# Last layer pair in 2x2 blocks with seven block products in place of eight, its weights kept in DRAM

## Chip, core and metric

The kernel runs on one core of a Trainium2 chip. The metric is the device time of one execution in microseconds. The core's engines work side by side and meet by semaphores: TensorE (PE, with its weight load PEld) does the matmuls, VectorE (DVE) and ScalarE (ACT) do elementwise work and empty PSUM, where matmuls leave their sums, GpSimd (POOL) gathers and scatters rows, SyncE (SP) issues most of the DMAs. Each engine takes its instructions in a fixed order.

## What is computed

Attention over 8 batches and 8 heads gives x of 4608 rows (tokens) and 512 columns. A router gives each of 8 experts 576 tokens, and each expert computes `relu(x @ w1[e]) @ w2[e]`. The change concerns the last pair of layers:

```python
def _moe2_ref(x, w1, w2, w3, w_out) -> np.ndarray:
    h = np.maximum(np.maximum(x @ w1, x @ w2), x @ w3)
    return (h @ w_out).astype(np.float32)
```

with w1, w2, w3 of 512 x 768 and w_out of 768 x 512. These four matrices come as 64-bit floats.

## The kernel before

**Split products.** Each fp32 operand is split into a high part of type fp32r and a low part, the rest. A product is three matmuls on TensorE, high·high, low·high and high·low, for each 128 rows of the contraction.

**Stages.** Attention and the first part of the routing take the time to about 210 us. Then the 8 experts run one after another (r = 0 to 7), each with a first matrix (line L891: 8 tiles f of 128 features, in two halves of 288 tokens and 12 matmuls each) and a second (L921: 4 tiles d, 24 matmuls in each half). A tile of the first matrix is emptied by ACT (L900, relu and high part, `hhi`) and DVE (L908, low part, `hlo`). A tile of the second is emptied by ACT into `ys` (L928) and sent to `yd` in DRAM by a DMA that ACT issues (L929). `acc` has two buffers in PSUM, so that tile d+2 can't start before tile d has been emptied. The stage starts for expert 7 at 621.55 us, its second matrix at 646.99 us, and the last layer pair at 672.43 us.

**Last pair.** `yd` is read back in 9 blocks b of 512 tokens (`yload`, L846) and split (`ysplit`, L857). `layer1(b, f)` does the three products of one tile f of 128 features (m = 0, 1, 2 for w1, w2, w3; L974, 12 matmuls of 512 columns each): 9 x 6 x 3 x 12 = 1944 matmuls. Their maximum is taken by ACT (L980) and DVE (L982, L983), and split (L985, L986). `layer2(b, t)` multiplies 128 tokens by w_out (L996, 18 matmuls of 512 columns), 36 x 18 = 648 matmuls, and is followed by a copy (L1000) and a scatter by GpSimd (L1002). The split weights of this stage stay in SBUF, 12 chunks of 1 MB.

**Weights and conversion.** Chunks of weights come from DRAM into `raw` (L657), are split by ACT (L672) and DVE (L679), and lie in a ring of 11. The 64-bit weights are converted on the chip by `convert()`: 24 jobs of 128 x 512 numbers, each an ACT operation (L785), six DVE operations (L788 to L803) and a store to DRAM (L806: `m0` to `m2`, `mo`), from which they come back as ordinary chunks.

**What sets the order.** The order on each engine is written by the program. `pump()`, called after each 6 matmuls of the experts, asks a planner which pending piece of splitting, routing or conversion may come next: a `Clock` counts what is booked on DVE against the time of TensorE, and a conversion step is placed where it fits within a limit. `have(n)` forces chunk n where it is needed.

Of the kernel before, what the change touches and what calls it, by code (L numbers as in the profile page):

```python
# [20 lines left out]
G = NT // 128  # L21
NU = G // 4
# [586 lines left out]
def kernel(ctx, tc, q, k, v, w_gate, w1, w2, m1, m2, m3, m_out, out, mark=lambda n: None):  # L609
# [6 lines left out]
    ms = [dram.tile([DM, F2], F32, name="m%d" % i) for i in range(3)] + [dram.tile([F2, DM], F32, name="mo")]  # L616
# [6 lines left out]
    ring = ctx.enter_context(tc.tile_pool(name="ring", bufs=11))  # L623
    P = rt.W = ctx.enter_context(tc.tile_pool(name="mw", bufs=1))
    PS = ctx.enter_context(tc.tile_pool(name="mps", bufs=2, space=PSUM))
    chunks = []
    todo, inflight, stage = [], [], ["raw%d" % i for i in range(4)]

    for n in stage:
        P.tile([128, 1024], F32, name=n)  # L630
    for n, w in (("xhi", 4), ("xlo", 4), ("hhi", 8), ("hlo", 8)):
        P.tile([128, w, CAP], F32R, name=n)
    NC = 8 * E + 12
# [16 lines left out]
    def issue():  # L650

        n = state["issued"]
        if todo and len(inflight) + len(half) < len(stage) and n - state["used"] < 11 + (n == NC - 1) and state["conv"] >= todo[0][2]:
            ap, a, _ = todo.pop(0)
            raw = P.tile([128, 1024], F32, name=stage[0])
            stage.append(stage.pop(0))
            nc.sync.dma_start(raw.rearrange("p (a f) -> p a f", a=a), ap)  # L657

            inflight.append([raw, clock.pe + (16 if state["issued"] % 8 == 0 else 10) * clock.PLACE])
            state["issued"] += 1  # L660

    def split_hi():
        mark("wsplit")
        raw, _ = inflight.pop(0)
        if state["split"] < NC - 1:
            t = ring.tile([128, 2, 1024], F32R, name="chunk")
            hi, lo = t[:, 0], t[:, 1]
        else:
            while half:
                split_lo()  # L670
            hi, lo = (P.tile([128, 1024], F32R, name="last%d" % i, tag=stage.pop(0)) for i in range(2))
# [32 lines left out]
    def gather(r):  # L704
        mark("gather")
        xg = []
        for t in range(5):
            g = P.tile([128, DM], F32, name="xg", bufs=5)
# [51 lines left out]
    def convert():  # L760


        jobs = [(src[a:a + 128, o:o + 256], dst[a:a + 128, o:o + 256]) for o in range(0, F2, 256)
                for src, dst in zip((m1, m2, m3), ms) for a in range(0, DM, 128)]
        jobs = [jobs[i:i + 2] for i in range(0, len(jobs), 2)]
        jobs += [[(m_out[a:a + 128, :], ms[3][a:a + 128, :])] for a in range(0, F2, 128)]
        raw, there = [], []

        def load(job):
            raw.append(P.tile([128, 512, 2], I32, name="c64", bufs=2))  # L770
            there.append(clock.pe + 10 * clock.PLACE)
            n = 512 // len(job)
            for i, (ap, _) in enumerate(job):
                nc.sync.dma_start(raw[-1][:, i * n:i * n + n].rearrange("p f w -> p (f w)"), ap.bitcast(I32))

        load(jobs[0])
        for i, job in enumerate(jobs):
            yield 270, there[i]
            mark("conv")
            if i + 1 < len(jobs):  # L780
                load(jobs[i + 1])
            hw, lw = raw[i][:, :, 1], raw[i][:, :, 0]
            t = P.tile([128, 512], I32, name="ct", bufs=2)
# [7 lines left out]
            nc.vector.tensor_scalar(t, t, 3, 0x3FFFFFF8, op0=OP.logical_shift_left, op1=OP.bitwise_and)  # L791
            yield 540, 0
# [4 lines left out]
            nc.vector.tensor_scalar(hw, t, -0x800000, None, op0=OP.bitwise_and)  # L797
            yield 540, 0
# [4 lines left out]
            nc.vector.tensor_tensor(tf, ex, tf, op=OP.add)  # L803
            n = 512 // len(job)
            for k, (_, dst) in enumerate(job):
                nc.sync.dma_start(dst, tf[:, k * n:k * n + n])  # L806
            state["conv"] += 2
# [33 lines left out]
    NB = NT // 512  # L841
    YS = {}

    def yload(b):
        t = P.tile([128, 4, 512], F32, name="yraw", tag="aoh")
        nc.sync.dma_start(t, yd[:, b * 512:(b + 1) * 512].rearrange("(a p) t -> p a t", p=128))  # L846
        return t

    def ysplit(b, raw):
        mark("ysplit")  # L850
        if b % 2:
            t = P.tile([128, 2, 4, 512], F32R, name="yodd", tag="hhi")
            YS[b] = t[:, 0], t[:, 1]
        else:
            YS[b] = [P.tile([128, 4, 512], F32R, name="y" + n, tag=n) for n in ("xhi", "xlo")]
        for a in range(4):
            nc.scalar.copy(YS[b][0][:, a], raw[:, a])  # L857
            nc.vector.tensor_tensor(YS[b][1][:, a], raw[:, a], YS[b][0][:, a].bitcast(F32), op=OP.subtract)

# [8 lines left out]
    for r in range(E):  # L868
        if r + 1 == E:
            for i in range(3):  # L870
                for n, m in enumerate(ms[:3]):
                    want(m.rearrange("(a p) f -> p a f", p=128)[:, :, 256 * i:256 * i + 256], 4, 12 * i + 4 * n + 4)
            for i in range(3):
                want(ms[3].rearrange("(a p) f -> p a f", p=128)[:, 2 * i:2 * i + 2, :], 2, 36 + 4 * i + 4)
# [4 lines left out]
        for f in range(8):  # L879
# [4 lines left out]
            for hf in range(2):  # L884
# [21 lines left out]
                if hf == 1:  # L906
# [3 lines left out]
                    clock.book(1, 600)  # L910
        for d in range(4):
# [136 lines left out]
```

## Time and profile before

| | |
|---|---|
| median of 3 runs | 1273.55 us (1272.87 to 1275.11) |
| the profiled execution: its own time | 1270.92 us |
| its span in the trace | 1269.1 us |
| TensorE busy | 1230.4 us, 97% of the span |
| VectorE, ScalarE, GpSimd busy | 51%, 31%, 11% |
| experts, from about 210 us | to 672.43 us |
| last layer pair | 672.43 to about 1260.9 us |

The span is 1.8 us shorter than the profiled execution's own time, and that execution is 2.6 us below the median. The chain of waits shows what ended last at each moment; a timeline shows one engine's instructions by start and length; windows show the busy time of each engine in a stretch. In a timeline a row's length counts the pipeline of the last matmul in it, so the rate of matmuls is read from one row's start to the next.

### The profile page before, as it was taken

The numbers are of one execution on the slowest core, as the hardware profiler recorded it, in microseconds if no ns is written. First come the engines' busy times: TensorE is split into PE (matmuls) and PEld (weight loads), VectorE is DVE, ScalarE is ACT, GpSimd is POOL, SyncE is SP. The second block draws the span as 40 slices with busy tenths as digits, with TensorE's granted clock in tenths as the row PEclk, the third lists the DMA queues.
The fourth block names the chain that finished last, engine by engine and source line by source line (L and its number), as shares of the span: only waits on it lengthen the run. The fifth ranks groups of instructions, "written<-read, shape, count | busy, mean of one in ns | idle before, by whom it ended". The sixth has DMA issues, their size and how long they took to land.

```text
span 1269.1 us, 20900 instructions
## 1 busy us (share of the span) xinstructions
PE 1230.4 (97%) x8585; PEld 1075.4 (85%) x8585; DVE 649.5 (51%) x1359; ACT 398.3 (31%) x622; POOL 143.2 (11%) x239
## 2 busy tenths in 40 slices
PE   5999978999999999999999999999999999999997
PEld 4888855999999999999998888888888888888886
DVE  6888876777778687777664313131313131313121
ACT  4888832233333323354243212021211121212110
POOL 7222211012010010210000010101010101010101
PEclk9999987999999999999999999999999999999999
DMA  9999715364435353585652101010101010100000
GB/s 210 247 252 250 193 51 159 99 188 126 146 124 172 125 172 111 187 277 183 221 177 102 34 34 34 34 34 34 34 34 34 34 34 34 34 34 1 25 9 34
DMA packets 138017, 136.78 MB, mean 108 GB/s; under 512 B 37570, under 2 KB 114626, under 8 KB 137922
## 3 DMA queue, kind: packets, MB, share of 16 engines
q1 hardware_dynamic: 122514, 94.39, 27.2%
q0 software_dynamic: 9984, 31.47, 7.4%
q10 hardware_dynamic: 5424, 9.59, 2.0%
q8 instruction: 68, 1.11, 0.4%
q14 instruction: 27, 0.22, 0.1%
HBM read 100.75 MB, written 34.67 MB: 107 GB/s over the span
## 4 chain that ended last, share of the span: by engine, by line
PE 55%; issue 34%; DVE 6%; POOL 2%; DMA 1%; ACT 1%; POOLq 0%; SPq 0%; DVEq 0%; ACTq 0%
PE acc L921 15%; PE acc L891 14%; PE acc L974 6%; PE pX L166 3%; PE pT L95 3%; PE pc L974 3%; PE pS L116 3%; PE po L996 2%; POOL out_dram L1002 2%; PE pA L153 1%; PE pxt L732 1%; PE pY L184 1%; PE rp L487 1%; PE pL L196 1%; DVE hlo L908 1%
## 5 line engine op out<-in xcount | busy, mean ns | idle before, releaser
L921 PE MATMUL acc<-hhi,chunk 128*128 128x288 f32 x1024 | 212.8, 301 | 0.0
L891 PE MATMUL acc<-xhi,chunk 128*128 128x288 f32 x1024 | 204.9, 300 | 2.2 <-DVE hlo L908 1.3
L891 PEld LDWEIGHTS acc<-xhi,chunk 128*128 128x128 f32 x1024 | 160.3, 188 | 3.8 <-DVE hlo L908 2.3
L921 PEld LDWEIGHTS acc<-hhi,chunk 128*128 128x128 f32 x1024 | 162.6, 188 | 0.1
L982 DVE TENSOR_TENSOR tb<-ta,acc 128x512 f32<-128x512 f32 x54 | 37.1, 687 | 234.0 <-ACT ta L980 233.9
L921 PE MATMUL acc<-hlo,chunk 128*128 128x288 f32 x512 | 150.9, 295 | 0.1
L974 PE MATMUL acc<-yxhi,chunk 128*128 128x512 f32 x480 | 147.8, 389 | 0.0
L891 PE MATMUL acc<-xlo,chunk 128*128 128x288 f32 x512 | 143.1, 295 | 0.0
L974 PE MATMUL acc<-yodd,chunk 128*128 128x512 f32 x576 | 134.4, 389 | 0.0
L974 PEld LDWEIGHTS acc<-yodd,chunk 128*128 128x128 f32 x576 | 108.1, 188 | 22.5
L1002 POOL DMA_INDIRECT out_dram<-ot,ia x36 | 34.6, 962 | 673.9 <-DVE ot L1000 621.0
L974 PEld LDWEIGHTS acc<-yxhi,chunk 128*128 128x128 f32 x480 | 90.1, 188 | 18.8
L679 DVE TENSOR_TENSOR chunk<-raw,chunk 128x1024 fp32r<-128x1024 f32 x75 | 91.0, 1218 | 23.8 <-ACT chunk L672 23.4
L921 PEld LDWEIGHTS acc<-hlo,chunk 128*128 128x128 f32 x512 | 96.0, 188 | 0.3 <-DVE hlo L908 0.3
L980 ACT COPY ta<-acc 128x512 f32<-128x512 f32 x54 | 31.7, 586 | 204.6 <-PE acc L974 202.5
L891 PEld LDWEIGHTS acc<-xlo,chunk 128*128 128x128 f32 x512 | 93.4, 188 | 0.0
L974 PE MATMUL acc<-yxlo,chunk 128*128 128x512 f32 x240 | 93.4, 389 | 0.0
L900 ACT ACTIVATE hhi<-acc 128x576 fp32r<-128x576 f32 x64 | 41.8, 653 | 140.4 <-PE acc L891 125.5
L672 ACT CAST chunk<-raw 128x1024 fp32r<-128x1024 f32 x75 | 77.3, 1047 | 18.2 <-ACT ys L928 8.4
L996 PE MATMUL po<-chunk,hm 128*128 128x512 f32 x324 | 79.3, 389 | 0.0
L709 POOL DMA_INDIRECT xg<-xd,idx x40 | 40.0, 999 | 316.1 <-DVE ohe L597 158.5
L983 DVE TENSOR_TENSOR tb<-tb,pc 128x512 f32<-128x512 f32 x54 | 37.1, 687 | 73.3 <-PE pc L974 73.2
(203 smaller groups left out, 1888.6 us busy)
## 6 DMA issues: line engine op xcount, KB each, us to landing
raw<-in_moe_w_dram SPq DMA_DIRECT2D x64, 512.0 KB, 4.6
xd<-x POOLq DMA_DIRECT2D x36, 256.0 KB, 6.0
c<-in_moe_w_dram SPq DMA_DIRECT2D x36, 256.0 KB, 4.7
yd<-ys ACTq DMA_DIRECT2D x32, 288.0 KB, 3.6
yraw<-yd SPq DMA_DIRECT2D x9, 1024.0 KB, 5.1
vb<-in_v_dram SPq DMA_DIRECT2D x112, 64.0 KB, 6.0
m<-ct SPq DMA_DIRECT2D x36, 128.0 KB, 2.4
raw<-m SPq DMA_DIRECT2D x9, 512.0 KB, 6.2
```

Of the source, the lines that this page charges most:

```text
L95: nc.tensor.transpose(pt[:, a, w, :], QK[nm, u][:, h, w * 128:w * 128 + 128], ident)
L116: nc.tensor.matmul(ps[c * 64:(c + 1) * 64, hp, :], QT[u][:, hp, 2 * h + c, :], KB[u % 2][:, 2 * h + c, hp].rearrange("p s i -> p (s i)"), ...
L166: nc.tensor.matmul(PX[g][c * 64:(c + 1) * 64, hp, :], AT[g][:, hp, c * 64:c * 64 + 64], VB[u % 3][:, 2 * h + c, hp].rearrange("p s i -> p ...
L672: nc.scalar.copy(hi, raw)
L679: nc.vector.tensor_tensor(lo, raw, hi.bitcast(F32), op=OP.subtract)
L709: nc.gpsimd.indirect_dma_start(out=g, out_offset=None, in_=xd[:, :], in_offset=bass.IndirectOffsetOnAxis(ap=rt.idx[r][:, t:t + 1], axis=0))
L891: nc.tensor.matmul(acc[:, hf, :288], w[a][:, dc, o:o + 128], x[:, dc, tk], start=n == 0, stop=n == 11)
L900: nc.scalar.activation(hv, acc[:, :, :288], AF.Relu)
L921: nc.tensor.matmul(acc[:, hf, :288], w[a][:, f, :], x[:, f, tk], start=n == 0, stop=n == 23)
L974: nc.tensor.matmul(ps, w[a][:, dc, o:o + 128], x[:, dc], start=n == 0, stop=n == 11)
L996: nc.tensor.matmul(po, h[:, x, t * 128:t * 128 + 128], w[a][:, f % 2], start=n == 0, stop=n == 17)
L1002: st = nc.gpsimd.indirect_dma_start(out=out, out_offset=bass.IndirectOffsetOnAxis(ap=ia[:, 4 * b + t:4 * b + t + 1], axis=0), in_=ot, in_o ...
```

## The change

**Seven products.** The last pair takes 6 super-blocks s of 768 tokens in place of 9 of 512. In one super-block a step g (9 of them: 3 pairs of feature tiles times m = 0, 1, 2) computes a 2x2 block product: 256 features in two halves, 768 tokens in two halves of `TB` = 384, the contraction of 512 in two halves. In place of eight half-size products it forms seven, from sums of weight blocks (`pool` operations on GpSimd in `convert()`, once for each weight) and differences of token blocks (`xprep`, once in each super-block, with new names `xb`, `xt`). A product is 6 matmuls of 384 columns: 6 x 9 x 7 x 6 = 2268 matmuls. `layer2` keeps its 648 matmuls; all its copies go to ACT.

**Sums in PSUM and outside.** Four PSUM names (`px`, `py`, `pz`, `po`, one bank and two buffers each) replace `acc` and the others in this stage. Products p1 to p7 accumulate there or are added by DVE; `best` takes the maximum over m, `low` splits the result.

**Weights from DRAM.** The conversion ends in seven blocks (`cw`), each split by ACT (`pair_hi`) and DVE (`pair_lo`) and stored in DRAM as `wda` and `wdb`, 384 and 512 KB for each of 18 jobs. Each g loads its weights anew: `wload_a` 0.79 MB and `wload_b` 1.05 MB, two buffers each, 54 times. Only w_out's 3 chunks stay in SBUF; 9 of 12 chunk splits go, the ring has 10 places, and the conversion's tiles `ct`, `cw` and `pair` have one buffer each.

**The conversions' end.** All conversion steps that the planner hasn't placed are issued between the two matrices of expert 7; behind them the loads of the first weights and tokens.

```diff
...
+        def pair_hi(job):
+            mark("conv")
+            job["pair"] = P.tile([128, 7, 2, 128], F32R, name="pair")
+            nc.scalar.copy(job["pair"][:, :, 0], job["cw"])
+            return clock.pe + 2 * clock.PLACE
...
+            pair = job["pair"]
+            nc.vector.tensor_tensor(pair[:, :, 1], job["cw"], pair[:, :, 0].bitcast(F32), op=OP.subtract)
...
+            nc.sync.dma_start(wda[row:row + 128, dc], flat[:, :768])
+            nc.sync.dma_start(wdb[row:row + 128, dc], flat[:, 768:])
...
+            pool = nc.gpsimd.tensor_tensor
+            pool(cw[:, 4], cw[:, 0], cw[:, 3], op=OP.add)
+            pool(cw[:, 5], cw[:, 1], cw[:, 0], op=OP.subtract)
+            pool(cw[:, 0], cw[:, 3], cw[:, 5], op=OP.subtract)
+            pool(cw[:, 6], cw[:, 2], cw[:, 0], op=OP.subtract)
+            job = {"at": at, "cw": cw}
...
+        if r + 1 == E:
+            while state["next"]:
+                convert_one()
+            for g in range(2):
+                wload_a(g)
+            yload(0)
...
+            if r + 1 == E:
+                if d == 0:
+                    have(NC)
+                    for g in range(2):
+                        wload_b(g)
+                xprep(*(("b11", "t2", "b21"), ("t1",), ("t3", "t4"), ("b22",))[d])
...
+        for dc in range(2):
+            for a, c in ((0, 0), (1, 0), (0, 1)):
+                nc.tensor.matmul(dst, w[:, dc, o, a], XO[x][:, c, dc], start=start and n == 0, stop=stop and n == 5,
+                                 skip_group_check=True)
+                n += 1
...
+    def p1(g):
+        XB[g] = PS.tile([128, 512], F32, name="px")[:, :TB]
+        product(g, XB[g], WA[g % 2], 1, "b11", True, False)
+        U[g, 1] = TMP[:, g % 2]
+        nc.scalar.copy(U[g, 1], XB[g])
+    def p6(g):
+        YZ[g] = [PS.tile([128, 512], F32, name=n)[:, :TB] for n in ("py", "pz")]
+        product(g, YZ[g][0], WA[g % 2], 0, "t2", True, False)
+        U[g, 2] = TMP[:, 2 + g % 2]
+        tt(U[g, 2], YZ[g][0], U[g, 1], op=OP.add)
+    def p4(g):
+        product(g, YZ[g][0], WB[g % 2], 0, "t4", False, True)
+        best(g, 1, 0, YZ[g][0], U[g, 1])
+    def p3(g):
+        product(g, YZ[g][1], WB[g % 2], 3, "b22", False, True)
+        wload_b(g + 2)
+        best(g, 0, 1, YZ[g][1], U[g, 2])
+    def p2(g):
+        product(g, XB[g], WA[g % 2], 2, "b21", False, True)
+        wload_a(g + 2)
+        best(g, 0, 0, XB[g])
+    def p5(g):
+        product(g, YZ[g][1], WB[g % 2], 1, "t1", True, False)
+    def p7(g):
+        product(g, YZ[g][0], WB[g % 2], 2, "t3", False, False)
+        u3 = TMP[:, 4 + g % 2]
+        tt(u3, YZ[g][0], U[g, 1], op=OP.add)
+        best(g, 1, 1, YZ[g][1], u3)
...
+    for s in range(NS):
+        for k in range(9):
+            g = 9 * s + k
+            p1(g)
+            p6(g)
+            if k:
+                low(g - 1, 1, 1)
+                p4(g - 1)
+                low(g - 1, 1, 0)
+                p3(g - 1)
+                low(g - 1, 0, 1)
+            p2(g)
+            low(g, 0, 0)
+            p5(g)
+            p7(g)
...
```

TensorE in the last pair. Before, the rows of one product (the last of `acc`, then `pc`, the third weight) run on, three kinds of matmul in turn:

```order
L974 MATMUL acc<-yxhi,chunk 128x512 x2
L974 MATMUL acc<-yxlo,chunk 128x512
L974 MATMUL acc<-yxhi,chunk 128x512 x2
L974 MATMUL acc<-yxlo,chunk 128x512
L974 MATMUL pc<-yxhi,chunk 128x512 [waits DVE_49]
L974 MATMUL pc<-yxhi,chunk 128x512
L974 MATMUL pc<-yxlo,chunk 128x512
```

After, from p1 of a step g to its p5: p1 writes `px`, p6 `py`, then p4 and p3 of the g before it, p2, p5 (DVE_49 is a wait for VectorE, DMAHW one for a DMA):

```order
L1029 MATMUL px<-xb_9017,wa_8952 128x384 [waits DMAHW1_49]
L1029 MATMUL px<-xb_9017,wa_8952 128x384 x5
L1029 MATMUL py<-xt_9022,wa_8952 128x384 [waits DVE_49]
L1029 MATMUL py<-xt_9022,wa_8952 128x384 x5
L1029 MATMUL py<-xt_9140,wb_9015 128x384 [waits DVE_49]
L1029 MATMUL py<-xt_9140,wb_9015 128x384 x5
L1029 MATMUL pz<-xb_9195,wb_9015 128x384 [waits DVE_49]
L1029 MATMUL pz<-xb_9195,wb_9015 128x384 x5
L1029 MATMUL px<-xb_9025,wa_8952 128x384 [waits Activation_49]
L1029 MATMUL px<-xb_9025,wa_8952 128x384 x5
L1029 MATMUL pz<-xt_9080,wb_9013 128x384 [waits DMAHW4_49]
L1029 MATMUL pz<-xt_9080,wb_9013 128x384 x5
```

Each product has 6 matmuls, and the first of nearly every one waits for an engine or a load; before, two waits stood in 36 matmuls.

ScalarE at the end of expert 7. Before, from the last relu (L900) to the first split of tokens (L857):

```order
L900 ACTIVATE hhi<-acc 128x576 [waits PE_49]
L672 CAST chunk<-raw_8861 128x1024 [waits DMAHW7_49]
L928 COPY ys<-acc 128x576 [waits PE_49]
L929 DMA yd<-ys 128x576 [waits Activation_49]
L672 CAST chunk<-raw_8928 128x1024 [waits DMAHW1_49]
L928 COPY ys<-acc 128x576 [waits DMAHW0_49,PE_49]
L929 DMA yd<-ys 128x576 [waits Activation_49]
L672 CAST chunk<-raw_8994 128x1024 [waits DMAHW5_49]
L928 COPY ys<-acc 128x576 [waits DMAHW4_49,PE_49]
L929 DMA yd<-ys 128x576 [waits DMAHW0_49,Activation_49]
L857 CAST yxhi<-yraw 128x512 [waits DMAHW3_49]
L857 CAST yxhi<-yraw 128x512 x3
```

After, from the last relu (L961) on; L807 and L782 belong to the conversion (first operation, `pair_hi`), L997 is the copy into `ys`, L921 `xprep`:

```order
L961 ACTIVATE hhi<-acc 128x576 [waits PE_49]
L807 ACTIVATE ct<-c_2705 128x512 [waits DMAHW1_49,DMAHW2_49,DMAHW0_49,DVE_49]
L782 CAST pair<-cw 128x7x128 [waits DMAHW3_49,DMAHW4_49,Activation_49,Pool_49]
L782 CAST pair<-cw 128x7x128 [waits DMAHW5_49,DVE_49,DMAHW6_49,Activation_49,Pool_49]
L997 COPY ys<-acc 128x576 [waits PE_49]
L998 DMA yd<-ys 128x576 [waits Activation_49]
L921 CAST xb_9017<-yraw_8956 128x768 [waits DMAHW4_49]
L921 CAST xt_9022<-tmp 128x768 [waits DVE_49]
L921 CAST xb_9025<-yraw_8958 128x768 [waits DMAHW5_49]
L997 COPY ys<-acc 128x576 [waits PE_49]
L998 DMA yd<-ys 128x576 [waits DMAHW0_49,Activation_49]
L921 CAST xt_9080<-tmp 128x768
```

Between the last relu and the first `ys` now stand the first operation of the last job and two `pair_hi`, each of which waits for GpSimd and for loads or stores; between the first `ys` and the second stand three splits of tokens, two of which wait for loads.

SyncE at the same place. Before, from the last pieces of conversion to the loads of tokens (`yraw`):

```order
L806 DMA mo<-ct 128x512
L657 DMA raw_8928<-m_62 128x4x256
L806 DMA mo<-ct 128x512
L846 DMA yraw<-yd 128x4x512
L657 DMA raw_8994<-m_63 128x4x256
L657 DMA raw_9051<-m_64 128x4x256
L846 DMA yraw<-yd 128x4x512
```

After, from the store of the last job but one on:

```order
L793 DMA wda<-pair 128x768 [waits DMAHW5_49,DVE_49]
L794 DMA wdb<-pair 128x1024 [waits DMAHW6_49]
L793 DMA wda<-pair 128x768 [waits DMAHW0_49,DVE_49]
L794 DMA wdb<-pair 128x1024 [waits DMAHW1_49]
L896 DMA wa_8952<-wda 128x1536 [waits DMAHW2_49,PE_49]
L896 DMA wa_8954<-wda 128x1536 [waits DMAHW3_49,PE_49]
L889 DMA yraw_8956<-yd 128x2x768 [waits DMAHW4_49]
L889 DMA yraw_8958<-yd 128x2x768 [waits DMAHW5_49]
L903 DMA wb_9013<-wdb 128x2048 [waits DMAHW6_49]
L903 DMA wb_9015<-wdb 128x2048 [waits DMAHW7_49]
```

The loads of weights and tokens stand behind the stores of the last job, each of which waits for VectorE.

## Rows read from the trace of the kernel before

**Rows 1.** The page: busy us, share of the span and instructions of TensorE and others.

```profile
PE 1230.4 (97%) x8585; PEld 1075.4 (85%) x8585; DVE 649.5 (51%) x1359; ACT 398.3 (31%) x622; POOL 143.2 (11%) x239
```

**Rows 2.** Chain of work that ended last, 560 to 740 us: start, length, what.

```profile
...
646.99 25.44 PE acc L921 x192
672.43 5.46 PE acc L974 x24
677.89 2.72 PE pc L974 x12
...
```

**Rows 3.** Timeline of TensorE: the first rows of two tiles of w_out in turn.

```profile
729.41 0.84 PE L996 MATMUL po<-chunk,he 128*128 128x512 f32 x3
...
733.52 0.84 PE L996 MATMUL po<-chunk,he 128*128 128x512 f32 x3
```

**Rows 4.** Lines by form, VectorE: out<-in, shape, count | busy us, mean ns | idle.

```profile
L679 DVE TENSOR_TENSOR chunk<-raw,chunk 128x1024 fp32r<-128x1024 f32 x75 | 91.0, 1218 | 23.8 <-ACT chunk L672 23.4 <-issue 0.3
L982 DVE TENSOR_TENSOR tb<-ta,acc 128x512 f32<-128x512 f32 x54 | 37.1, 687 | 234.0 <-ACT ta L980 233.9
L788 DVE TENSOR_SCALAR ct<-ct 128x512 f32<-128x512 f32 x24 | 10.3, 428 | 7.4 <-ACT ct L785 7.4
L386 DVE TENSOR_TENSOR t<-L,bid 128x288 f32<-128x288 f32 x7 | 3.2, 458 | 0.2
```

**Rows 5.** Lines by form, ScalarE (same columns).

```profile
L672 ACT CAST chunk<-raw 128x1024 fp32r<-128x1024 f32 x75 | 77.3, 1047 | 18.2 <-ACT ys L928 8.4 <-DMA raw<-mo 4.4 <-DMA raw<-in_moe_w_dram 2.8
L785 ACT ACTIVATE ct<-c 128x512 f32<-128x512 f32 x24 | 16.2, 673 | 0.8 <-ACT ys L928 0.5 <-DMA c<-in_moe_w_out_dram 0.3
L199 ACT COPY ls<-pL 128x384 f32<-128x384 f32 x1 | 0.5, 479 | 1.2 <-PE pL L196 1.2
```

**Rows 6.** Windows: busy us (count) of each engine, granted clock, DMA share, GB/s.

```profile
461.00:556.00 95.00, 94.21 (x833) 91.49 (x832) 71.72 (x165) 32.99 (x48) 15.96 (x21) 1.00 0.51 159
556.00:672.00 116.00, 116.00 (x882) 116.00 (x880) 80.02 (x118) 49.04 (x68) 0.00 (x0) 1.00 0.63 204
704.00:705.00 1.00, 1.00 (x6) 0.82 (x5) 0.00 (x0) 0.00 (x0) 0.00 (x0) 1.00 1.05 408
800.00:900.00 100.00, 100.00 (x442) 82.62 (x442) 24.11 (x36) 16.76 (x29) 8.38 (x16) 1.00 0.10 34
```

**Rows 7.** DMA issues: queue, count, KB each, median us from issue to landing.

```profile
yraw<-yd SPq DMA_DIRECT2D x9, 1024.0 KB, 5.1
mo<-ct SPq DMA_DIRECT2D x6, 256.0 KB, 2.3
```

**Rows 8.** Timeline of ScalarE around the end of expert 7.

```profile
...
653.39 0.64 ACT L928 COPY ys<-acc 128x576 f32<-128x576 f32 x1 [4.77 <-PE acc L921]
...
659.75 0.64 ACT L928 COPY ys<-acc 128x576 f32<-128x576 f32 x1 [4.27 <-PE acc L921]
...
```

**Rows 9.** Windows around a wait of TensorE before the experts (columns as Rows 6).

```profile
185.00:205.00 20.00, 15.04 (x142) 7.28 (x142) 13.23 (x60) 0.94 (x2) 0.00 (x0) 0.50 0.14 46
205.00:210.00 5.00, 5.00 (x23) 2.61 (x22) 3.88 (x10) 2.05 (x2) 3.71 (x4) 0.70 0.96 330
```

**Rows 10.** Lines by form and timelines, GpSimd and (one row) VectorE: arithmetic and copies.

```profile
L340 POOL TENSOR_TENSOR blk<-blk 128x64 f32<-128x64 f32 x1 | 0.3, 319 | 0.1
L342 POOL TENSOR_TENSOR blk<-blk 128x32 f32<-128x32 f32 x1 | 0.3, 252 | 0.1
...
517.48 1.29 POOL L715 COPY ia<-idx 128x4 int32<-128x4 int32 x1
...
517.18 1.21 DVE L679 TENSOR_TENSOR chunk<-raw,chunk 128x1024 fp32r<-128x1024 f32 x1
...
414.47 0.22 POOL L715 COPY ia<-idx 128x4 int32<-128x4 int32 x1
```

**Rows 11.** Timeline of GpSimd: the gather of expert 7's rows.

```profile
541.20 0.97 POOL L709 DMA_INDIRECT xg<-xd,idx  x1 [22.30 <-PE pxt L732]
...
550.98 0.18 POOL L719 COPY ia<-idx 64x4 int32<-64x4 int32 x1 [3.08 <-DMA xg<-xd,idx]
```

More of the change, by code (lines that the diff above doesn't have):

```diff
@@ L664, in split_hi @@
         raw, _ = inflight.pop(0)
[L665 to L671, printed above, removed]
+        t = ring.tile([128, 2, 1024], F32R, name="chunk")
+        hi, lo = t[:, 0], t[:, 1]
         nc.scalar.copy(hi, raw)
@@ L779, in convert @@
+        load(0)
+        job = None
+        for i, (kind, at) in enumerate(jobs):
+            yield 0, there[i]
             mark("conv")
             if i + 1 < len(jobs):
-                load(jobs[i + 1])
-            hw, lw = raw[i][:, :, 1], raw[i][:, :, 0]
-            t = P.tile([128, 512], I32, name="ct", bufs=2)
+                load(i + 1)
+            hw, lw = c64[:, i % 2, :, 1], c64[:, i % 2, :, 0]
+            t = P.tile([128, 512], I32, name="ct")
             tf, ex = t.bitcast(F32), hw.bitcast(F32)
@@ L802, in convert @@
             mark("conv")
[L803 to L807, printed above, removed]
+            cw = P.tile([128, 7, 128], F32, name="cw")
+            c4 = cw[:, 0:4].rearrange("p a f -> p (a f)")
+            nc.vector.tensor_tensor(c4, ex, tf, op=OP.add)
+            if job:
+                store(job)
+                job = None
+            if kind == "o":
+                nc.sync.dma_start(mo[128 * at:128 * at + 128, :], c4)
+                state["conv"] += 1
+                continue
+            pool = nc.gpsimd.tensor_tensor
[4 more added lines that the diff above has]
+            job = {"at": at, "cw": cw}
+        yield 0, clock.pe + 3 * clock.PLACE
+        yield 900, pair_hi(job)
+        pair_lo(job)
+        store(job)
     def convert_one():
@@ L988, in layer2, with hview @@
[L988 to L997 removed]
+    def hview(f):
+        return HT[f // 3][:, f % 3]
@@ new lines, in product, with best @@
+    def product(g, dst, w, o, x, start, stop):
+        mark("mmB")
+        n = 0
+        for dc in range(2):
[3 more added lines that the diff above has]
+                n += 1
+    def best(g, i, j, a, b=None):
+        m = g % 3
+        M = MX[:, i, j]
+        if m == 0:
+            if b is None:
+                nc.scalar.copy(M, a)
+            else:
+                tt(M, a, b, op=OP.add)
+        elif b is None:
+            tt(M, M, a, op=OP.max)
+        else:
+            c = CT[:, nct[0] % 2]
+            nct[0] += 1
+            tt(c, a, b, op=OP.add)
+            tt(M, M, c, op=OP.max)
+        if m == 2:
+            nc.scalar.copy(hpart(g, i, j)[0], M)
@@ L998, in layer2 @@
+    PO = {}
+    def layer2(t, fs):
+        if t not in PO:
+            PO[t] = PS.tile([128, 512], F32, name="po")
+        for f in fs:
+            w, h = WO[f // 2], hview(f)
+            mark("mmO")
+            for n, (a, x) in enumerate(((0, 0), (1, 0), (0, 1))):
+                nc.tensor.matmul(PO[t], h[:, x, t % 6 * 128:t % 6 * 128 + 128], w[a][:, f % 2],
+                                 start=f == 0 and n == 0, stop=f == 5 and n == 2)
+        if fs[-1] != 5:
+            return
         mark("out")
```

225 lines of the change are left out of this document (112 added, 113 removed).

## Prediction

> **What bounds the kernel now.** I read the page first: TensorE is busy for 97% of the span [rows 1]. The chain of waits says where that binds: over the last pair (672.43 us to the end) it is TensorE alone, one product behind the other, and so it is for the second matrix of expert 7 [rows 2]. A product of 12 matmuls of 512 columns takes 2.72 us, 226.7 ns each; the first of the third weight's 12 waits for VectorE, yet its product takes no longer, so a wait that is met costs nothing. Two tiles of w_out start 4.11 us apart [rows 3]. The windows say that the other engines have room there: in 800 to 900 us VectorE is busy for 24.1 of 100 us, ScalarE 16.8, and DMA moves 34 GB/s [rows 6]. So here the number and length of matmuls count, as long as nothing else gets into the chain. In the expert stage TensorE is as full (94.21 of 95 us), but VectorE is busy for 71.72 of them (75%) [rows 6]: there is little room for more conversion.
>
> **Matmuls, the gain.** Removed: 1944 x 226.7 ns = 440.7 us. Added: 2268 of 384 columns, a shape with no row of this kind. 192 of 288 columns take 25.44 us, 132.5 ns each [rows 2]; a straight line to 226.7 ns gives 172.9 ns at 384, so 392.1 us and a gain of 48.5 us. In proportion to columns from the row of 512 it is 170.0 ns (gain 55), from that of 288 176.7 ns (gain 40). I take the line, since the cost for each matmul is in both rows. A product is then 1.04 us, a step g 7.26 us. The 648 matmuls of w_out stay at 36 x 4.11 = 148 us. The Trainium skill, page "TensorE: Matmul & The Clock Gate", section "Back-to-back issue gap", gives columns at 2.4 GHz plus about 2.5 ns; by that 384 columns take 162.5 ns and 512 take 215.8, and the gain would be 51 us. The rows lie some 11 ns above it, and the sum goes by the rows.
>
> **The steady state: what must stay hidden.** VectorE has 5, 9 and 13 operations of 128 x 384 in steps of m = 0, 1, 2. By line from 458 ns (288 columns) to 687 ns (512) [rows 4] one takes 556 ns: 27 x 0.556 = 15.0 us in three steps of 21.8 us, 69%. ScalarE copies 384 columns in 479 ns [rows 5], at most 6 in a step. What could wait is the ring of one step: p7 ends, VectorE adds (`u3`), and p4 two products (2.07 us) later writes the same bank. Behind a step with m = 2 VectorE still works off its 13 operations; laid out one behind the other, with 0.2 us from the end of the last matmul's turn to its result (three matmuls of 0.68 us last 0.84 [rows 3]) and under 0.1 for each handing over (the first `ys` starts 0.04 us behind its tile's turn [rows 8]), `u3` comes 0.4 us before p4 at 556 ns, and 0.5 us too late in two of nine steps at 600 ns (6 us in all). Taken +1, range 0 to 8. Between super-blocks `xprep` (eleven VectorE operations of 768 columns, about 0.95 us each) lies beside six tiles of w_out, 24.7 us: nothing.
>
> Weights: 1.835 MB for each step, in 7.26 us: 253 GB/s for the whole stage, where it was 34. The trace reaches 408 and 410 GB/s in single microseconds [rows 6], so it takes 4.5 us, and two buffers leave 8 to 9 us from a load's issue to its use. Nothing, with a rival below. The token loads (1.57 MB in each of five super-blocks) add 3.9 us to 90 and find that room.
>
> **Expert stage.** Added: 18 `pair_lo` of 896 columns, between 687 and 1218 ns, by line 1.09 us, so 19.5 us on VectorE; 18 `pair_hi` on ScalarE (about 0.93 us by the 1047 ns of 1024 columns [rows 5]); 72 additions on GpSimd, which did nothing here but gathers. Nine chunk splits go (11 us on VectorE). What matters is the queue of ScalarE: a `pair_hi` waits for four additions and, with one buffer `pair`, for the store before; relus and `ys` copies of TensorE's tiles stand behind it, and a relu may come some 2.5 us late (a tile of matrix one takes an eighth of 25.44 us, 3.18, a copy of 576 columns 0.64 [rows 8]) before TensorE stands. An addition of 128 x 128: 252 ns for 32 columns and 319 for 64 [rows 10] give about 450, four 1.8 us; hidden in most jobs. At one place it isn't: the gather for expert 7 holds GpSimd from 541.20 to past 550.98 us with 3.08 us of waiting for its DMA [rows 11]; additions caught behind it hold ScalarE for some 5 us, TensorE for 2 to 3. With 0.1 to 0.2 us for each other job: +5, range 0 to 15.
>
> **Handing over, the largest loss.** All conversion that isn't placed is issued behind matrix one of expert 7 (time T = 646.99). By the order that is the low part of job 21's pair, the end of job 22, all of job 23 but its load, and the pairs of 22 and 23. On ScalarE two `pair_hi` stand in front of the first `ys`. Chain: relu and low part about 1.5 us; `pair_lo` 1.1; two stores of job 21 issued and landed (256 KB take 2.3 us [rows 7], 384 + 512 KB some 4 to 5), since `pair` has one buffer: 7.5; `pair_hi`, `pair_lo` of job 22, two VectorE operations of 0.69: 11; additions 1.8, and the store of 22 landed: 14 to 15; `pair_hi` 0.9: 15 to 16. Before, `ys` of d = 0 came at T + 6.40 and of d = 1 at T + 12.76 [rows 8], and d = 2 wants its bank at T + 12.72. Now it starts at about T + 16.7.
>
> The second `ys` waits longer: in front of it stand three token splits, and the token loads are on SyncE behind the last store, which is issued at T + 17 to 18. From there 0.92 MB of stores, 1.57 MB of weights and 1.57 MB of tokens go at 400 GB/s: 10 us, landed by T + 29 to 30 (with the 1 MB load's 5.1 us from issue to landing [rows 7] as a check, for less data). Then two subtractions on VectorE (0.95 each) and two copies on ScalarE (0.82 each), `ys`: T + 33 to 34.5. Tile d = 3, due at T + 19.1, starts at about T + 34 and ends at T + 40.5 in place of 25.44: +15. The first `px` likely waits for the last copy of `acc`: +0.9. After a stand of some 10 us the clock: in 185 to 205 us, with TensorE busy for 15 of 20 us, the granted clock is 0.50, the 1.2 GHz level, and comes back in the five us after 205 (0.70) under an unbroken row of matmuls [rows 9]; some 5 us at half speed cost +2.5 (0 to 4). In all 18.4, and 0.5 for the last relu behind a `pair_hi`: +19. From below: if two fewer steps are left to issue and loads land at once, d = 3 is held only by three copies, +8; from above, loads at three quarters of that rate and stores that land 2 us later each, +28.
>
> **Tail.** The last tile's copy and scatter stay as they are: 0.
>
> **Sum.** -48.5 + 1 + 5 + 19 = -23.5 us on a profiled time of 1270.92: 1247.4. The median shown is 2.6 us above it: 1250.
>
> **Rivals.**
> 1. *The gain comes nearly whole.* The forced steps are few, token loads land early, and the clock holds: handover +8, the rest 0 to 2: 1233 to 1235. For it: DMA's share of its time is 0.63 or less before [rows 6]; against: the loads stand in SyncE's order behind a store that waits for VectorE, which no spare bandwidth mends.
> 2. *GpSimd and VectorE get in each other's way.* A 128 x 4 copy on GpSimd took 1.29 us beside a 1.21 us subtraction of VectorE, and 0.22 us in another place [rows 10]. If each addition waits like that (+1.07 us), four take 6.1 us and not 1.8, and a `pair_hi` holds ScalarE 0.5 to 1 us beyond what relus can bear: 18 x 0.75 = 13 us more, 1263. Also VectorE, at 75%, may wait in its turn. The Trainium skill, page "SBUF — State Buffer", section "Who interferes with whom", says the two share one pair of ports under an exclusive lock, and that the later one blocks until the first ends. The pair of rows at 517 us agrees, the one at 414 us shows no such wait.
> 3. *Slower: VectorE's answer to p7 sets the step.* If an operation of 384 columns takes as long as one of 512 (687 ns), `u3` comes 2.05 us late in two of nine steps: 12 x 2.05 = 25 us, which eats the gain; the point is at about 680 ns. With the handover at its upper end: 1280. Against it: both shapes with rows scale with columns.
> 4. *Slower: the weights don't arrive.* Below 253 GB/s each step waits; at 238 GB/s (7.70 us a step) the gain is gone, at 200 GB/s it costs 54 x 1.9 = 103 us: 1353. For it: no row shows such a stream for 400 us; against: 408 and 410 GB/s in the single rows, 204 GB/s as a mean over 116 us beside a busy TensorE [rows 6].
> 5. *No change seen*, with handover and experts both at their upper ends (28 + 15): -48.5 + 44 + 1, 1270.
>
> **How the numbers follow.** The forecast (handover 12 to 25, experts 0 to 10): 0.55. Rival 1: 0.14; rival 2: 0.15; rival 5: 0.05; rival 3: 0.06; rival 4: 0.05. A measurement of this kernel tells about 0.2%, 2.5 us, from no change. Faster by more: forecast, 1, 2 = 0.84; same: 0.05; slower: 0.11. The range: from rival 1 (1232) up past rival 2 with its handover some us longer (1268); rivals 3, 4 and 5 lie outside.
>
> **What would show it.** Matmuls of the last pair start 173 ns apart, a step lasts 7.26 us, a super-block about 90 us, and the last pair 540 us, in the timeline of TensorE. Tiles d = 2 and 3 of expert 7 wait for ScalarE's `ys`, by 4 and 11 us more, the second with the token split before it waiting for a DMA. The granted clock dips behind it. The first matmuls of p4 wait for VectorE, for nothing or some tenths. Experts 6 and 7: 25.44 us for each matrix, or more where a relu stands behind `pair_hi`. What would make it wrong: a spacing of 384 columns off the line, weights that land after their use, GpSimd additions far above 0.45 us, or a handover whose loads came early.

## The result, and the profile after

The changed kernel takes 1252.64 us (1250.94 to 1254.28, 4 runs), the kernel before 1273.66 beside it: a ratio of 0.9834 (95% interval 0.9817 to 0.9851). The forecast was 1250 us, the range 1232 to 1268. The profiled execution took 1250.94 us, its span is 1249.2. The page, whose second line answers to [rows 1] (busy us, share, instructions):

```profile
span 1249.2 us, 22278 instructions
...
PE 1190.4 (95%) x8909; PEld 1109.2 (89%) x8909; DVE 842.1 (67%) x1704; ACT 433.3 (35%) x691; POOL 190.2 (15%) x311
```

By stages of the two traces, each stage counted from the start of its first matmul (for expert 7's second matrix before that is 646.83 us; the chain's 646.99 is the end of the matmul ahead of it):

| stage | before, us | after, us | difference | forecast |
|---|---|---|---|---|
| start to the end of expert 7's first matrix | 646.8 | 657.7 | +10.9 | +5 (0 to 15) |
| from there to the first product of the last pair | 25.4 | 42.2 | +16.8 | +19 (8 to 28) |
| last pair, first to last matmul | 588.7 | 541.0 | -47.6 | -47.5 |
| from there to the end | 8.2 | 8.2 | 0 | 0 |
| span | 1269.1 | 1249.2 | -19.9 | -23.5 |

**The last pair** runs as one row of matmuls. The timeline of TensorE (start, length, 6 matmuls to a row):

```profile
705.25 1.20 PE L1029 MATMUL px<-xb,wa 128*128 128x384 f32 x6
706.29 1.20 PE L1029 MATMUL py<-xt,wa 128*128 128x384 f32 x6
707.33 1.20 PE L1029 MATMUL py<-xt,wb 128*128 128x384 f32 x6
708.37 1.20 PE L1029 MATMUL pz<-xb,wb 128*128 128x384 f32 x6
```

The rows start 1.04 us apart, 173.3 ns for each matmul. From 705 us to the last matmul TensorE waits for no other engine and no load. VectorE's operation took what the line between two shapes gave (lines by form; count, busy us, mean ns, idle and releaser):

```profile
L1093 DVE TENSOR_TENSOR tmp<-py,tmp 128x384 f32<-128x384 f32 x54 | 30.0, 556 | 48.3 <-PE py L1029 48.3
```

**The handing over** reads off the chain of waits (start, length, what), to be set beside [rows 2, 8]:

```profile
...
655.49 3.47 DMA wdb<-pair
659.06 0.95 ACT pair L782
...
661.26 1.09 DVE pair L788
...
662.77 3.17 DMA wdb<-pair
666.05 0.95 ACT pair L782
...
667.03 1.10 DVE pair L788
...
668.51 3.16 DMA wdb<-pair
...
671.77 0.95 ACT pair L782
672.74 1.10 DVE pair L788
...
676.47 8.41 DMA yraw<-yd
684.90 0.84 ACT xb L921
...
686.64 0.96 DVE tmp L915
687.62 0.97 DVE tmp L916
...
690.77 8.46 PE acc L990 x48
699.25 0.65 ACT ys L997
...
699.94 1.31 PE px L1029 x6
```

With matrix one ending at T = 657.7, the last `pair_hi` starts at T + 14.1, behind three stores that each take 3.2 to 3.5 us to land (the first of them, issued just before T, is that of job 20); the first `ys` follows at T + 14.9. The token loads, issued behind the last store, land at T + 27.2. Then come the copy and the low part of the first split, two subtractions, two more copies, the second `ys`, and d = 3 at T + 33.1, due at T + 19.1. It takes 8.5 us in place of 6.36. The windows say why (columns as Rows 6):

```profile
565.00:570.00 5.00, 3.99 (x31) 3.75 (x29) 1.66 (x3) 1.56 (x2) 0.69 (x1) 1.00 0.96 341
570.00:575.00 5.00, 4.08 (x20) 4.09 (x21) 4.61 (x6) 2.60 (x4) 0.94 (x1) 0.69 0.49 194
575.00:580.00 5.00, 1.91 (x10) 1.68 (x9) 4.18 (x7) 2.13 (x3) 2.26 (x4) 0.84 0.92 264
580.00:585.00 5.00, 5.00 (x32) 5.00 (x31) 1.90 (x4) 1.81 (x3) 1.79 (x4) 0.78 0.81 287
685.00:690.00 5.00, 0.00 (x0) 0.00 (x0) 3.31 (x4) 2.12 (x3) 0.00 (x0) 0.50 1.03 427
690.00:695.00 5.00, 4.23 (x18) 4.24 (x19) 3.43 (x5) 2.92 (x5) 0.00 (x0) 0.52 0.47 190
800.00:900.00 100.00, 100.00 (x545) 95.70 (x544) 60.18 (x104) 21.27 (x39) 6.52 (x12) 1.00 0.63 232
```

TensorE stood still before 690.77 us; the granted clock is 0.50 in the five us before 690 and 0.52 behind, the lower of its two levels (1.2 GHz). The first four windows are those of the loss around expert 6: 7 of the 10.9 us lie in its first matrix, 33.0 us in place of 26.0 from its first matmul's start to its last one's end, and 1.8 in the wait just ahead of it. ScalarE there (timeline; in brackets the idle time before and its releaser):

```profile
...
568.44 0.94 ACT L782 CAST pair<-cw 128x896 fp32r<-128x896 f32 x1 [5.15 <-DMA wdb<-pair]
...
570.23 0.63 ACT L997 COPY ys<-acc 128x576 f32<-128x576 f32 x1
...
577.45 0.94 ACT L782 CAST pair<-cw 128x896 fp32r<-128x896 f32 x1 [2.82 <-POOL cw L844]
578.30 0.63 ACT L997 COPY ys<-acc 128x576 f32<-128x576 f32 x1
...
```

and TensorE:

```profile
...
570.92 1.48 PE L952 MATMUL acc<-xhi,chunk 128*128 128x288 f32 x8 [1.93 <-ACT ys L997]
...
578.98 0.85 PE L952 MATMUL acc<-xhi,chunk 128*128 128x288 f32 x2 [3.09 <-ACT ys L997]
...
```

A `pair_hi` waits 5.15 us for the store of the job before; the `ys` copy behind it in ScalarE's order is late, and TensorE waits 1.93 us for its bank. The next one costs 3.09 us; there the last thing that `pair_hi` waited for was GpSimd's fourth addition (`cw`, L844). The granted clock behind the waits is 0.69, 0.84 and 0.78. Together the 5.0 us of waiting cost 8.7: from the start of expert 5's second matrix to that of expert 6's second pass 62.1 us (from 541.55 us) where it was 53.4. The rest of the 10.9 lies in expert 6's second matrix (1.2) and before 515 us (0.9).

### The profile page after: what moved, and what is told of

The parts are those of the page before. It is cut to its first block, busy times and chain, and to the rows that moved or that the text cites. A ratio compares the mean times of both kernels' runs of the same rounds, so it can differ in the third digit from the quotient of the medians.

```text
span 1249.2 us, 22278 instructions
## 1 busy us (share of the span) xinstructions
PE 1190.4 (95%) x8909; PEld 1109.2 (89%) x8909; DVE 842.1 (67%) x1704; ACT 433.3 (35%) x691; POOL 190.2 (15%) x311
## 4 chain that ended last, share of the span: by engine, by line
PE 53%; issue 29%; DVE 8%; DMA 4%; POOL 3%; ACT 2%; SPq 1%; POOLq 0%; DVEq 0%; ACTq 0%
PE acc L990 12%; PE acc L952 12%; PE py L1029 4%; PE pX L168 3%; PE px L1029 3%; PE pz L1029 3%; PE pT L97 3%; PE pS L118 3%; PE po L1105 3%; POOL out_dram L1113 2%; DMA wdb<-pair 1%; PE pA L155 1%; PE pxt L733 1%; PE pY L186 1%; DVE chunk L680 1%
## 5 line engine op out<-in xcount | busy, mean ns | idle before, releaser
L1105 PE MATMUL po<-chunk,h 128*128 128x512 f32 x648 | 149.3, 390 | 0.0
L1105 PEld LDWEIGHTS po<-chunk,h 128*128 128x128 f32 x648 | 121.4, 188 | 24.8
L1029 PE MATMUL px<-xb,wa 128*128 128x384 f32 x648 | 129.9, 334 | 0.7 <-ACT ys L997 0.7
L1029 PE MATMUL py<-xt,wb 128*128 128x384 f32 x648 | 129.8, 334 | 0.0
L1029 PEld LDWEIGHTS px<-xb,wa 128*128 128x128 f32 x648 | 114.0, 188 | 1.4 <-ACT ys L997 1.0
L1029 PEld LDWEIGHTS py<-xt,wb 128*128 128x128 f32 x648 | 114.0, 188 | 0.5
L1050 ACT CAST h<-best 128x384 fp32r<-128x384 f32 x72 | 37.0, 513 | 198.2 <-DVE best L1048 121.3
L680 DVE TENSOR_TENSOR chunk<-raw,chunk 128x1024 fp32r<-128x1024 f32 x67 | 82.4, 1232 | 6.6 <-DMA raw<-in_moe_w_dram 3.7
L961 ACT ACTIVATE hhi<-acc 128x576 fp32r<-128x576 f32 x64 | 41.7, 652 | 120.4 <-PE acc L952 110.4
L1065 ACT COPY tmp<-px 128x384 f32<-128x384 f32 x54 | 25.9, 479 | 146.2 <-PE px L1029 146.2
L1029 PE MATMUL py<-xt,wa 128*128 128x384 f32 x324 | 64.8, 334 | 0.0
```

The lines of the kernel that those rows point to most:

```text
L680: nc.vector.tensor_tensor(lo, raw, hi.bitcast(F32), op=OP.subtract)
L961: nc.scalar.activation(hv, acc[:, :, :288], AF.Relu)
L1029: nc.tensor.matmul(dst, w[:, dc, o, a], XO[x][:, c, dc], start=start and n == 0, stop=stop and n == 5, skip_group_check=True)
L1105: nc.tensor.matmul(PO[t], h[:, x, t % 6 * 128:t % 6 * 128 + 128], w[a][:, f % 2], start=f == 0 and n == 0, stop=f == 5 and n == 2)
```

## The experiments

Four change the handing over, three the expert stage, three load the steady state. Ratios are to the kernel before, run on the same chip; the changed kernel's is 0.9834. The diffs are shortened; square brackets stand for several lines.

**Token loads ahead (h_loads).**

```diff
 if r + 1 == E:
+    have(NC)
+    yload(0)
     while state["next"]:
         convert_one()
     for g in range(2):
         wload_a(g)
-    yload(0)
```

> One part moved alone: the loads of the first tokens are issued before the forced conversion steps between the two matrices of expert 7 (their second half goes to the raw1 space, the second wb buffer to c64), the rest stays. Theory 1 (tile d = 3 waits because the token loads stand on SyncE behind the last store): the tokens lie in SBUF by about 665 us, the second ys comes about 5 us behind the first, at 678, the wait of 9.3 us before d = 3 goes and the low clock behind it: 11 to 12 us less than the changed kernel, about 1241 us. Theory 2 (what holds d = 3 is DMA bandwidth that stores and weights take): the tokens land as late as before and the time stays at 1252.6 us.

1243.11 us, ratio 0.9767 (0.9751 to 0.9783): 8.5 us less by ratio, where theory 1 said 11 to 12. No wait before d = 3 is left, as theory 1 says. But d = 2 now waits 7.35 us for the first `ys` (1.94 in the changed kernel): the loads have gone ahead of stores that ScalarE waits for. ScalarE and, below, TensorE:

```profile
...
671.57 0.94 ACT L782 CAST pair<-cw 128x896 fp32r<-128x896 f32 x1 [7.03 <-DMA wdb<-pair]
...
```

```profile
...
678.88 0.85 PE L991 MATMUL acc<-hhi,chunk 128*128 128x288 f32 x2 [7.35 <-ACT ys L998]
...
```

The store that this `pair_hi` waits for was issued at 662.96 us, behind the token loads at 658.32, and took 8.5 us in place of 3.2. Part of the gain was given back in that way.

**Splits behind the second copy (h_order).**

```diff
-xprep(*(("b11", "t2", "b21"), ("t1",), ("t3", "t4"), ("b22",))[d])
+xprep(*((), ("b11", "t2", "b21"), ("t1",), ("t3", "t4", "b22"))[d])
```

> One part moved alone: the first three token splits are written behind the second ys copy instead of ahead of it; loads and conversions stay. Theory 1 (d = 3 itself needs nothing of the tokens, it waits by ScalarE's order): no wait before d = 3, which starts behind d = 2 at about 680 us; then the first product waits for the token splits, until about 691 us where it started at 699.9: 8 to 9 us less, about 1244 us. Theory 2 (the loads bound the handing over, the order on ScalarE only shows where): the first product starts as late as before, within 2 us, and the time stays at 1251 to 1253 us.

1251.8 us, ratio 0.984 (0.9824 to 0.9856): no change in the time, as in theory 2. ScalarE and, below, the first products:

```profile
...
675.08 0.64 ACT L997 COPY ys<-acc 128x576 f32<-128x576 f32 x1 [0.40 <-ACT ys L997]
...
687.29 0.83 ACT L921 CAST xb<-yraw 128x768 fp32r<-128x768 f32 x1 [11.57 <-DMA yraw<-yd]
...
694.25 0.63 ACT L997 COPY ys<-acc 128x576 f32<-128x576 f32 x1
```

```profile
...
694.93 2.29 PE L1029 MATMUL px<-xb,wa 128*128 128x384 f32 x6 [7.20 <-ACT ys L997]
...
700.95 2.12 PE L1029 MATMUL px<-xb,wa 128*128 128x384 f32 x6 [2.37 <-ACT tmp L1065]
...
```

The second `ys` is done at 675.7 us and d = 3 waits for nothing, but the tokens land at 687.29, and the first product waits 7.2 us and runs at the low clock. It starts at 694.93 us, 5.0 us sooner than in the changed kernel, where theory 2 had 2 at most; but the remaining splits are then still to do, p2 waits another 2.37 us behind them, and the granted clock is 0.72 and 0.66 from 695 to 705 us. From the first product to the last matmul it takes 546.6 us in place of 541.0, which gives the gain back. The order on ScalarE only showed where the late loads were felt.

**All of it at once (h_both).**

```diff
-while state["next"]: convert_one()
-for g in range(2): wload_a(g)
+have(NC)
 yload(0)
+for g in range(2): wload_a(g)
+wload_b(0)
 ...
-xprep(*(("b11", "t2", "b21"), ("t1",), ("t3", "t4"), ("b22",))[d])
+xprep(*(("b11", "t2"), ("b21", "t1"), ("t3",), ("t4", "b22"))[d])
+if d == 3: [remaining conversion steps, wload_b(1)]
```

> All of the handing over changed: token and first weight loads ahead of the remaining conversion steps, these not forced but placed by the planner among the second matrix of expert 7, the token splits spread over its four tiles. If the conversions fit into its 25.4 us, the first product starts about 26.5 us behind matrix one (42.2 in the changed kernel): 15 to 16 us less, about 1237 us. If ScalarE's copies are held by pair_hi waiting for stores and additions, a wait of 2 to 4 us before d = 2 or d = 3 stays: 1240 to 1242 us.

1247.4 us, ratio 0.98 (0.9784 to 0.9817): worse than moving the token loads alone, a miss. ScalarE, and SyncE's issues before it:

```profile
...
678.21 0.94 ACT L782 CAST pair<-cw 128x896 fp32r<-128x896 f32 x1 [11.81 <-DMA wdb<-pair]
```

```profile
...
658.92 0.91 SPq L889 DMA_DIRECT2D yraw<-yd  x2
659.91 0.89 SPq L896 DMA_DIRECT2D wa<-wda  x2
660.86 0.67 SPq L903 DMA_DIRECT2D wb<-wdb  x1
663.12 0.32 SPq L793 DMA_DIRECT2D wda<-pair  x1
663.49 0.42 SPq L794 DMA_DIRECT2D wdb<-pair  x1
```

Five loads, 4.2 MB, are issued from 658.92 to 661.5 us, the stores of job 21 at 663.12 and 663.49. At 427 GB/s 4.2 MB take 9.8 us; the store has landed only at 678.2, and `pair_hi` holds ScalarE for 11.81 us. DMA is not idle in between: from 666 to 674 us the windows read 414 to 430 GB/s.

**Stores freed (x_storefree).**

```diff
-nc.sync.dma_start(wda[row:row + 128, dc], flat[:, :768])
-nc.sync.dma_start(wdb[row:row + 128, dc], flat[:, 768:])
+nc.sync.dma_start(wda[row:row + 128, dc], other[:, :768])   # rows of xd
+nc.sync.dma_start(wdb[row:row + 128, dc], other)
```

> Leaves out that the converted weights reach DRAM: the two stores of each job copy other rows of DRAM, as many bytes, so pair_hi no longer waits for the store before it. Theory 1 (the loss in expert 6 comes from ScalarE waiting for that store with one pair buffer): the waits of 1.9 and 3.1 us of TensorE at 571 and 579 us go, expert 6's first matrix takes 26 us and not 33, and the forced steps get shorter by 0 to 3 us: 7 to 10 us less, 1243 to 1246 us. Theory 2 (it comes from GpSimd's additions): pair_hi then waits for those, expert 6's first matrix loses 3 us or more: at most 3 us less, 1250 us.

1236.04 us in one run (span 1234.2, 15 us less than the changed kernel's). Expert 6's first matrix takes 28.6 us; matrix one of expert 7 ends 7.0 us sooner, and the handing over takes 34.3 us. The direction of theory 1 holds, its figures (1243 to 1246 us, no wait left) don't: one wait of 1.70 us stays, at 573.83, behind a `pair_hi` that waits 1.58 us for GpSimd, and the handing over is 8 us shorter, not 0 to 3. Those 8 us aren't the landing's alone: stores that wait for no `pair` are issued at once, and so the token loads behind them go at T + 6.1 in place of T + 18.8.

**Additions on VectorE (x_adds_dve).** `pool = nc.vector.tensor_tensor` in place of `nc.gpsimd.tensor_tensor`.

> The four additions of each conversion job are done by VectorE in place of GpSimd, at the same place of the program; the rest stays as in the changed kernel (ratio to the kernel before 0.9834). Theory 1 (GpSimd's additions, which took up to 1.3 us each beside VectorE's subtractions, hold pair_hi and so TensorE): four take about 1.2 us, the second wait of expert 6's first matrix (3.1 us) goes, the forced steps get 1 to 2 us shorter: 4 to 6 us less than the changed kernel, ratio 0.979 to 0.980. Theory 2 (the wait for the store with one buffer is what counts, and VectorE is nearly full): the wait at 571 us stays or grows, relus' low parts come later: within 2 us of the changed kernel or slower, ratio 0.982 or more.

1249.64 us, ratio 0.9817 (0.9801 to 0.9834), an interval that overlaps that of the changed kernel: theory 2. The waits of TensorE at 571 and 578 us are 1.76 and 2.53 us. The quarrel over the additions is real, though. GpSimd and, below, VectorE in the changed kernel:

```profile
...
574.06 1.31 POOL L841 TENSOR_TENSOR cw<-cw 128x128 f32<-128x128 f32 x1 [8.37 <-DVE cw L831]
...
580.99 0.46 POOL L841 TENSOR_TENSOR cw<-cw 128x128 f32<-128x128 f32 x1 [3.57 <-DVE cw L831]
```

```profile
...
573.83 1.22 DVE L680 TENSOR_TENSOR chunk<-raw,chunk 128x1024 fp32r<-128x1024 f32 x1
...
580.76 0.75 DVE L969 SCALAR_TENSOR_TENSOR hlo<-acc,hhi 128x576 fp32r<-128x576 f32 x1
```

Beside a subtraction of two SBUF operands an addition took 1.31 us, and 0.46 beside an operation that reads PSUM. About 10 of 72 additions take 1.28 us or more. It costs TensorE about 1 us: without them the `pair_hi` ahead of the second wait ends its waiting 0.5 us sooner, at 576.95, and then by the store; and expert 6's second matrix takes 27.4 us in place of 28.5.

**Two pair buffers (pair2).** `pair0` and `pair1` in turn, the ring with 9 places, the split `b22` in the space of `pair1`.

> The converted blocks get two pair buffers in place of one, so that a pair_hi waits for the store before the last; the space comes from the ring of chunks, 9 places in place of 10 (one token split lies in the second pair buffer later). Theory 1 (the store's landing with one buffer is what costs the experts and part of the handing over; with the stores freed it was 16.6 us): 1236 to 1240 us, expert 6's first matrix at 28 to 29 us. Theory 2 (a ring of 9 is too short, chunks come late): TensorE waits for chunk splits in several experts, 1245 us or more.

1243.57 us, ratio 0.9789 (0.9772 to 0.9805). Expert 6's first matrix takes 26.8 us, the loss there is gone, and no chunk comes late: on the experts theory 1. The handing over still takes 41.5 us, d = 3 waits 11.18 us for the token loads. The first `ys` still comes only at T + 13.5, though no `pair_hi` there waits for a store any more; the last one waits 4.58 us for the last job's own steps, which end with GpSimd's additions from 661.98 us on:

```profile
...
663.95 0.94 ACT L782 CAST pair<-cw 128x896 fp32r<-128x896 f32 x1 [4.58 <-POOL spacer L1112]
...
```

So the total misses theory 1's range by 4 us: the second buffer without the earlier loads gains nothing there, the stores freed had also let the loads go sooner.

**Both causes removed (best1).** The two buffers, the token splits spread over the four tiles as in h_both, and:

```diff
 if r + 1 == E:
-    while state["next"]: convert_one()
-    for g in range(2): wload_a(g)
+    have(NC)
     yload(0)
 ...
+    if d == 0: [wload_a(0), wload_a(1)]
+    if d == 1: wload_b(0)
+    if d == 3: [remaining conversion steps, wload_b(1)]
```

> The two pair buffers, and the handing over as in the run with everything changed, but with the 4.2 MB of loads spread: the tokens' 1.6 MB ahead of the remaining conversion, the first weights behind tiles d = 0 and d = 1. If the stores' landing behind those loads was what held ScalarE there: no wait before d = 2 and d = 3 over 1 us, the first product 27 us behind matrix one, 1229 to 1233 us. If additions on GpSimd and VectorE's queue hold it as well: waits of 2 to 4 us, 1234 to 1238 us.

1227.79 us (1227.61 to 1227.9), ratio 0.9665 (0.9649 to 0.9681): it beats both kernels. The handing over takes 26.4 us, d = 2 and d = 3 wait for nothing; the first product:

```profile
...
676.15 1.31 PE L1033 MATMUL px<-xb,wa 128*128 128x384 f32 x6 [0.73 <-ACT ys L996]
```

**Two more operations in the ring (s_dve2).** `tt(u3, U[g, 1], U[g, 1], op=OP.add)` twice ahead of `u3`.

> Two more VectorE operations of 128 x 384 in each step, right ahead of u3, whose results are overwritten. By the ring laid out in the prediction p4 then waits 1.9 us in two of nine steps: 6 x 3.8 = 23 us more than the changed kernel, 1275 us, with TensorE's waits on VectorE at p4 of the first step behind each m = 2. By mean load alone (VectorE from 69% to 84% of a step) nothing waits: 1252 us.

1270.75 us in one run, span 1269.0, 20 us above the changed kernel's. All of TensorE's waits from 705 us on (sum, times, longest):

```profile
PE py L1029 <- DVE tmp L1095: 17.1, 12, 1.7
```

Twelve waits, all for `u3`, two in each super-block, those of the steps right behind its first and its second m = 2. The ring is as laid out, with 1.4 to 1.7 us a wait where 1.9 was worked out. Mean load would have let it pass.

**Twice the weights (s_stream2).** Each `dma_start` of `wload_a` and `wload_b` written twice.

> Every load of weights in the last pair is issued twice, 3.67 MB for each step in place of 1.835. If the stream is then bound by the 408 to 427 GB/s seen in single windows, a step takes 8.6 to 9.0 us in place of 7.28: 54 steps, 71 to 93 us more, 1324 to 1345 us. If 253 GB/s was already near what such a stream reaches, 14.5 us a step: over 1600 us.

1522.82 us in one run, outside both expectations, and it decides nothing on bandwidth: the second load into the same tile is issued some 6 us behind the first (a `wb` at 803.21 us, again only at 809.33), and the loads behind it on SyncE are late with it. That it waits for the first to land fits these times and is not shown apart.

**Other bytes beside the weights (s_extra).**

```diff
 nc.sync.dma_start(WB[g % 2]..., wdb[...])
+nc.sync.dma_start(junk[g * 128:g * 128 + 128, :], wdb[...])
```

> With each wb load of the last pair 1.05 MB more are copied from DRAM to DRAM, written nowhere that is used; no load waits for them but by the DMA queue. 2.88 MB for each step of 7.28 us are 396 GB/s, just under the 408 to 427 GB/s of single windows. If bandwidth is the only limit: no waits or some tenths of a us a step, 1250 to 1260 us. If a load has to land within its time behind such a copy and doesn't (2.6 us more in the queue): waits of 1 us or more a step, 1300 us or more.

1285.97 us in one run, span 1284.2, 35 us more, between the two. TensorE's waits, and a window:

```profile
PE px L1031 <- DMA wa<-wda: 23.6, 17, 3.2
PE pz L1031 <- DMA wb<-wdb: 2.7, 4, 1.3
```

```profile
710.00:760.00 50.00, 45.96 (x262) 45.00 (x261) 29.96 (x56) 7.54 (x16) 0.00 (x0) 1.00 0.94 366
```

DMA is busy for 0.94 of the time and moves 366 GB/s: in this run the mixture of loads and copies from DRAM to DRAM goes no further, below the 408 of single microseconds. The kernel's own 232 GB/s (800 to 900 us) at a share of 0.63 has room.

## Why the prediction was right, and where it was off

The forecast was 1250 us and 1252.64 came. That the total is so near is in part luck: the terms were off by +5.9 us (experts) and -2.2 (handing over), which offset each other.

- **Matmuls**: 172.9 ns from the line between two shapes, 173.3 measured; over 2268 matmuls that is 0.9 us, so 47.6 of the gain of 48.5 is there. The Trainium skill, page "TensorE: Matmul & The Clock Gate", section "Back-to-back issue gap", gives the prediction's 162.5 ns for a matmul by itself, and says that in a stream of weight loads and matmuls both set the spacing. The prediction used it for such a stream, and it is 11 ns low there, as for the other shapes.
- **Steady state**: +1 was 0; 556 ns for an operation was 556. The ring has little slack, which two more operations showed; rival 3 fell on the length of the operation alone.
- **Weights**: nothing waited, rival 4 fell. With copies from DRAM to DRAM as the added bytes the margin ends under 396 GB/s, not at 408; for loads alone its end was not found.
- **Handing over**: chain, order and places came as written: first `ys` at T + 14.9 (15 to 16), tokens at T + 27.2 (29 to 30), d = 3 at T + 33.1 (34), the clock's price in d = 3 2.1 us (2.5). The size was 2 us too large, and that the places agree is partly errors that offset each other. The chain starts with a store more than was counted, that of job 20, which holds the last relu (priced at 0.5) and makes `pair_lo` 2 us late; stores landing in 3.2 to 3.5 us and not in 4 to 5 made up for it. The tokens were put at T + 29 to 30 where the prediction's own terms (last store at T + 17 to 18, then 10 us) give T + 27 to 28, as measured; and from there to d = 3 it took 5.9 us in place of 4.2, since the first split's copy and low part stand ahead of the subtractions. That the loads' place and the one buffer count is shown by removing each alone and both: 8.5 and 5.7 us by ratio, and 21.5 together, with the conversion spread as well. The buffer's part lies in the expert stage: the handing over alone takes 42.2 us, with the loads ahead 36.4, with two buffers 41.5, with all of it 26.4. What of the rest is the spreading of the conversion and what that of the loads was not tried apart.
- **Experts**: the mis-sized term, 5 against 10.9. The step that failed is its cause: I let GpSimd's additions behind the gather hold ScalarE. They didn't; the gather was over when the next additions began, at 553.29 us. What held it was the other wait named in the same paragraph, the store with one buffer, which I priced only in the handing over. Here it lands late (6.7 us from issue to landing before 568.44, against 3.2 to 3.5 in the handing over); chunk loads are on the way at the same time, with a DMA share of 0.96 from 565 to 570 us, and that they are the reason was not tried apart. Freed, or with two buffers, expert 6's first matrix loses 0.8 to 2.5 us instead of 7. The sum also had the clock's price only in the handing over; behind expert 6's waits it is 3.7 us (8.7 less 5.0).
- **Rival 2**: the mechanism of ports is there in the rows, the price is not: some 2 us by ratio (0.9817 without it, 0.9834 with it, intervals that overlap), about 1 us in the stages, where 13 were worked out. The Trainium skill, page "SBUF — State Buffer", section "Who interferes with whom", has that mechanism; the rows at 574 and 581 us agree with it.

## What to carry to other kernels

A saving on the busiest engine comes whole where nothing else enters the chain; what it costs lies at the seams, so follow there each engine's order and ask what stands ahead of the copy that frees a bank. A single buffer that is stored to DRAM makes the next writer wait for the landing, and bulk loads issued just before lengthen that wait: buffer it twice, and put the loads that end a wait first, the others later. Check loops with slack in tenths of a us by adding work to them, not by mean load.

## What the hardware showed that was not expected

- The granted clock fell to 0.69, 0.84 and 0.78 in windows with and behind waits of only 1.9 and 3.1 us in a row of matmuls, so that 5 us of waiting cost 8.7. With a wait of 1.7 us at 730 us in s_dve2 it stayed at 1.00 (725 to 735 us).
- A 0.9 MB pair of stores landed 3.2 to 3.5 us after its second issue in the handing over, and 14.6 us after it behind 4.2 MB of loads (h_both).
- DMA with mixed loads and copies stood at 366 GB/s with its engines 0.94 busy, while a five-us window of loads (685 to 690 us) reached 427.
